# Turning gathered token rows through DRAM and VectorE instead of TensorE, from the third expert on

## The chip, the cores and the metric

The kernel runs on one core of a Trainium2 chip. The metric is the device time of one execution in microseconds (us); lower is better.

## What is computed

Sigmoid attention over 8 batches of 12 heads (448 tokens, head dimension 64), and then a mixture of 8 experts over the 3584 tokens of width 768. Each token goes to one expert; an expert holds at most 448 tokens, and the choice is greedy over all token-expert logits in descending order. Everything is float32.

```python
scores = scale * np.matmul(q, k.transpose(0, 1, 3, 2)) - np.log(S)
attn = 1.0 / (1.0 + np.exp(-scores))
x = np.matmul(attn, v)          # then transposed and reshaped to [3584, 768]
logits = x @ w_gate
...                             # greedy assignment, cap = N // E = 448
for e in range(E):
    mask = assigned == e
    h = np.maximum(x[mask] @ w1[e], 0.0)      # 768 -> 1024
    out[mask] = h @ w2[e]                     # 1024 -> 768
```

## The kernel before, in words

The first 275 us or so are attention (lines 363 to 531). Its rows are written to a DRAM tile `xs` of [3584, 768] (`rows`, L487 to L493). A router (class `Router`, L114 to L332) finds one full expert per phase: VectorE runs a search of 16 steps over the logits (L168 to L215), each step three counting instructions (L173) and a few small ones, and TensorE does small transposes and matmuls for it (L162, L224, L252, L257, L284, L291). A phase ends with the list of the expert's 448 tokens, `r_idx` (L293). The step numbered kx in the program is the expert found in phase kx; "expert 2" below is kx = 2, the third one.

For each expert the mixture stage then does this:

- `gather` (L616) reads the listed rows of `xs` into four SBUF tiles `xr` of up to 128 tokens (three of 128, one of 64) by indirect DMAs that GpSimd (POOL) issues.
- `xturn` (L621 to L636) turns them: channels have to lie on partitions for the matmul. Per tile and half of the channels, TensorE transposes three blocks of 128 channels into one PSUM tile `tp` (L632), ScalarE copies it, rounded, to `xh` (L635), and VectorE writes the remainder to `xl` (L636). That makes eight such groups per expert. A float32 product is made of three matmuls: high with high, low with high, high with low (L680, L682, L684; L715, L717, L719).
- `moe` (L660) runs the two weight stages. Stage 1 has four groups i of 256 hidden units, each made of two weight units (j = 0 uses channel blocks 0 to 2, j = 1 blocks 3 to 5). ScalarE evicts each group twice (L688 `hh`, L691 `yt`) and GpSimd writes the remainder `hl` (L692). Stage 2 has three groups of 256 output channels, evicted by ScalarE (L723). The PSUM pool `sc` has two buffers, so a third group can start only when the first has been evicted. `untranspose` (L641) turns the result back, two TensorE transposes per tile, with a ScalarE copy (L650), and GpSimd scatters finished rows (L653).
- Weights are streamed: `load_w` (L573) issues a DMA on the SP queue, three units ahead, and `split_w` (L592) makes the high part on ScalarE (L596) and the low part on GpSimd, for the last two experts on VectorE for every second unit (L598).

The order of the work is written out by the program, and each engine runs its own instructions strictly in that order. A generator `moe(kx)` yields after each matmul with an estimated cost; a clock adds these up. Routing steps are put in when the clock passes `t_route` (L772), and other pieces, the "chores", each with a due time, one per 1000 ns of that clock (L777 to L782). `prepare` (L752) makes the chores for the next expert as soon as its list has been emitted: gathers at `t0 + 1500 j`, turns later. `flush` runs what is left before the next expert begins.

```python
for j, n in blocks():
    for hf in range(2):
        chores.append((t0 + lag + 1500 * j, kx + 1,
                       lambda j=j, n=n, hf=hf: xturn(kx + 1, j, n, hf, False)))
```

Of the kernel before, what the change touches and what calls it, by code (L numbers as in the profile page):

```python
# [7 lines left out]
F32 = mybir.dt.float32  # L8
F32R = mybir.dt.float32r
# [4 lines left out]
AF = mybir.ActivationFunctionType  # L14
OP = mybir.AluOpType
# [3 lines left out]
STEP = 4.0e36  # L19
BIG = 16384.0  # L20
TWO23 = float(2 ** 23)
XR_BUFS = 12
XT_BUFS = 8
XA_BUFS = 4
AT_BUFS = 8
# [309 lines left out]
def moe_attention(tc, q, k, v, w_gate, w1, w2, out):  # L335
    nc = tc.nc
    B, H, S, D = q.shape
    DM = H * D
    E, _, F = w1.shape
    CP, NCH, NP, ND, NF = 112, S // 112, H // 2, DM // 128, F // 128  # L340
    G4 = 4
    PSUM = bass.MemoryType.PSUM
    with contextlib.ExitStack() as ctx:
# [229 lines left out]
        def load_w(u, behind=False):  # L573


            kx, st, i, j = units[u]
            if kx not in gate:
                gate[kx] = nc.sync.value_load(picked[kx][:1, :1], min_val=0, max_val=E - 1)
            t = wp.tile([128, 1024], F32, name="wr")
            if behind:  # L580
                nc.gpsimd.memset(t[:1, :1], 0.0)
            if st == 0:
                t = t[:, :768].rearrange("p (a f) -> p a f", a=3)
                src = w1[ds(gate[kx], 1)].rearrange("e (a p) f -> p (e a) f", p=128)
                nc.sync.dma_start(t, src[:, 3 * j:3 * j + 3, i * 256:(i + 1) * 256])
            else:
                t = t.rearrange("p (a f) -> p a f", a=4)
                src = w2[ds(gate[kx], 1)].rearrange("e (a p) f -> p (e a) f", p=128)
                nc.sync.dma_start(t, src[:, 4 * j:4 * j + 4, i * 256:(i + 1) * 256])
            raw[u] = t  # L590
# [17 lines left out]
                state["split"] += 1  # L608

        xg, XH = {}, {}  # L610

        def blocks():
            for j in range(4):
                yield j, min(128, S - 128 * j)

        def gather(kx, j, n):  # L616
            t = xg[kx, j] = xp.tile([128, DM], F32, name="xr", bufs=XR_BUFS)
            nc.gpsimd.indirect_dma_start(out=t[:n], out_offset=None, in_=xs,  # L618
                                         in_offset=bass.IndirectOffsetOnAxis(ap=listed[kx][:n, j:j + 1], axis=0))

        def xturn(kx, j, n, hf, wide):  # L621
            if (j, hf) == (0, 0):
                XH[kx] = (xp.tile([128, ND, S], F32R, name="xh", bufs=2),
                          xp.tile([128, ND, S], F32R, name="xl", bufs=2))
            xh, xl = XH[kx]
            if wide and hf:
                p = ps_s.tile([128, 2, 512], F32, name="sc")[:, 0]
            else:
                p = ps_t.tile([128, 512], F32, name="tp")
            for i in range(3):  # L630
                dd = hf * 3 + i
                nc.tensor.transpose(p[:, i * n:(i + 1) * n], xg[kx, j][:n, dd * 128:(dd + 1) * 128], ident[:n, :n])  # L632
            pv = p[:, :3 * n].rearrange("p (a t) -> p a t", a=3)
            sl = (slice(None), slice(hf * 3, hf * 3 + 3), slice(j * 128, j * 128 + n))
            nc.scalar.activation(xh[sl], pv, AF.Copy)  # L635
            nc.vector.tensor_tensor(xl[sl], pv, xh[sl].bitcast(F32), OP.subtract)  # L636
# [111 lines left out]
        for kx in range(E):  # L748
            turned = kx + 1 == E
            start = clock[0]  # L750

            def prepare():  # L752
                t0 = clock[0]
                lag = max(5000, min(14000, start + 40000 - t0))
                for j, n in blocks():
                    chores.append((t0 + 1500 * j, kx + 1, lambda j=j, n=n: gather(kx + 1, j, n)))
                for j, n in blocks():
                    for hf in range(2):
                        chores.append((t0 + lag + 1500 * j, kx + 1,
                                       lambda j=j, n=n, hf=hf: xturn(kx + 1, j, n, hf, False)))  # L760

            def flush(kx):
                for c in [c for c in chores if c[1] <= kx]:
                    chores.remove(c)
                    c[2]()

            for step, cost in enumerate(moe(kx)):
                clock[0] += cost
                t = clock[0]
                if kx == 0 and step == 35:  # L770
                    flush(0)
                if t >= t_route:  # L772
                    t_route = t + next(route, 0) + SLACK
                if not turned and kx + 1 in listed:
                    prepare()
                    turned = True
                if t >= t_chore:  # L777
                    c = next((c for c in chores if c[0] <= t), None)
                    if c:
                        chores.remove(c)  # L780
                        c[2]()
                        t_chore = t + CHORE_NS  # L782
            if not turned:
                while kx + 1 not in listed:
                    next(route)
                prepare()
            flush(kx + 1)
# [28 lines left out]
```

## Time and profile before

| what | us |
|---|---|
| three runs | 887.00, 890.27, 893.16 (median 890.27) |
| the profiled execution | 887.23 |
| its span, first to last instruction | 885.5 |
| mean granted TensorE clock | 0.984 |
| TensorE busy (PE) | 837.8 |
| VectorE busy (DVE) | 531.4 |
| ScalarE busy (ACT) | 456.2 |
| GpSimd busy (POOL) | 467.4 |

PE is matmul and transpose work, PEld the weight loads that overlap it, SP the queue that issues most DMAs. A row of the profile's timeline has the start, the duration, the engine, the line of the kernel, the operation, what it writes and reads, and, in brackets, how long the engine had been idle and what ended that. A row of the view of waits has what waited, for what, the total in us, the number of times and the longest. A row of the view by windows has the window, its length and, for each engine, the busy time and the number of instructions, then the granted clock, the share of time the DMA engines were busy and GB/s.

### The profile page before, as it was taken

To read this page: it belongs to the slowest core of one execution; us is meant where nothing else is said; L and a number is where in the kernel's file an instruction comes from. 1 tells how busy PE (TensorE), PEld (TensorE's weight loads), DVE (VectorE), ACT (ScalarE), POOL (GpSimd) and SP (SyncE) were. 2 spreads that over 40 slices of the span, in tenths; PEclk is the share of its full clock that TensorE was granted. 3 is DMA by queue.
4 is the path that set the end of the run, shared out by engine and by line. 5 is a ranking of instruction groups with operands and counts; after the bars stand their busy time and mean duration, and the time that the engine had idled before them with its cause. 6 is when DMAs were issued, how large, how long until landed. Compare 5 with 4: busy or idle time off the path is not lost.

```text
span 885.5 us, 16232 instructions
## 1 busy us (share of the span) xinstructions
PE 837.8 (95%) x5507; PEld 639.0 (72%) x5507; DVE 531.4 (60%) x2047; ACT 456.2 (52%) x610; POOL 467.4 (53%) x449
## 2 busy tenths in 40 slices
PE   6999999999998729998999999999999999999996
PEld 3455455455555518987988988988888888889996
DVE  4665555555554778958869779779689521421110
ACT  6777777777774724434424424434434434443431
POOL 9645444444400014846864964873883882752651
PEclk9999999999999969999999999999999999999999
DMA  9876666665603945434443542452552542632511
GB/s 172 168 144 127 132 125 123 131 126 120 138 12 100 299 161 153 136 107 161 136 133 117 146 156 75 157 164 95 153 164 70 178 146 72 228 111 72 192 49 63
DMA packets 203507, 117.57 MB, mean 133 GB/s; under 512 B 143936, under 2 KB 193088, under 8 KB 203424
## 3 DMA queue, kind: packets, MB, share of 16 engines
q1 hardware_dynamic: 190688, 83.03, 36.0%
q0 software_dynamic: 10880, 33.28, 11.9%
q8 instruction: 43, 0.70, 0.3%
q10 hardware_dynamic: 1856, 0.23, 0.2%
q14 instruction: 40, 0.33, 0.1%
HBM read 94.47 MB, written 22.02 MB: 132 GB/s over the span
## 4 chain that ended last, share of the span: by engine, by line
PE 77%; DVE 8%; DMA 5%; issue 4%; POOL 3%; ACT 1%; SPq 1%; POOLq 0%; ACTq 0%; DVEq 0%
PE tp L461 13%; PE sc L437 11%; PE sc L682 8%; PE sc L680 8%; PE sc L684 8%; PE sc L717 6%; PE sc L719 6%; PE sc L715 6%; PE tp L467 2%; DMA xs<-xr 2%; DVE r_junk L173 2%; PE sc L447 2%; PE tp L645 2%; DMA xr<-xs,r_idx 2%; PE tp L632 2%
## 5 line engine op out<-in xcount | busy, mean ns | idle before, releaser
L598 POOL TENSOR_TENSOR wl<-wr,wh 128x768 fp32r<-128x768 f32 (+1 forms) x96 | 205.9, 2155 | 134.6 <-ACT wh L596 126.9
L427 ACT ACTIVATE at<-sc,bias 128x896 f32<-128x896 f32 x168 | 161.0, 1006 | 63.1 <-PE sc L447 38.2
L372 POOL DMA_DIRECT2D nkq<-in_q_dram x188 | 118.6, 646 | 111.5 <-DVE kqT L412 104.7
L719 PE MATMUL sc<-hh,wl 128*128 128x448 f32 (+2 forms) x400 | 151.4, 378 | 0.0
L717 PE MATMUL sc<-hl,wh 128*128 128x448 f32 (+2 forms) x400 | 145.4, 364 | 0.1
L684 PE MATMUL sc<-xh,wl 128*128 128x448 f32 (+2 forms) x396 | 145.4, 367 | 0.0
L682 PE MATMUL sc<-xl,wh 128*128 128x448 f32 (+2 forms) x396 | 144.9, 366 | 0.0
L715 PE MATMUL sc<-hh,wh 128*128 128x448 f32 (+2 forms) x400 | 143.9, 360 | 0.0
L680 PE MATMUL sc<-xh,wh 128*128 128x448 f32 (+2 forms) x396 | 143.8, 363 | 0.0
L173 DVE TENSOR_SCALAR_CACHE_REDUCE r_junk<-r_KE,r_T 128x224 bf16<-128x224 f32 x315 | 123.2, 441 | 0.1
L461 PE MATMUL tp<-at,nv 128*64 128x448 f32 x576 | 118.8, 548 | 0.0
L596 ACT ACTIVATE wh<-wr 128x768 fp32r<-128x768 f32 (+1 forms) x112 | 102.0, 939 | 13.2 <-DMA wr<-in_moe_w_dram 13.1
L692 POOL TENSOR_TENSOR hl<-yt,hh 128x896 fp32r<-128x896 f32 x32 | 68.3, 2136 | 44.5 <-ACT yt L691 41.8
L421 DVE TENSOR_TENSOR kqL<-kqT,kqH 128x896 fp32r<-128x896 f32 (+1 forms) x49 | 52.6, 1073 | 58.3 <-ACT kqH L419 58.2
L688 ACT ACTIVATE hh<-sc 128x896 fp32r<-128x896 f32 x32 | 29.5, 920 | 111.0 <-PE sc L684 111.0
L618 POOL DMA_INDIRECT xr<-xs,r_idx x32 | 32.0, 1002 | 97.5 <-ACT wh L596 86.7
L717 PEld LDWEIGHTS sc<-hl,wh 128*128 128x128 f32 x400 | 75.2, 188 | 7.0 <-issue 1.1
L598 DVE TENSOR_TENSOR wl<-wr,wh 128x768 fp32r<-128x768 f32 (+1 forms) x16 | 25.1, 1571 | 91.7 <-ACT wh L596 91.5
L461 PEld LDWEIGHTS tp<-at,nv 128*64 128x64 f32 x576 | 37.1, 136 | 59.1 <-issue 57.9
L682 PEld LDWEIGHTS sc<-xl,wh 128*128 128x128 f32 x396 | 74.5, 188 | 6.3 <-issue 0.5
L715 PEld LDWEIGHTS sc<-hh,wh 128*128 128x128 f32 x400 | 75.6, 189 | 4.4
L680 PEld LDWEIGHTS sc<-xh,wh 128*128 128x128 f32 x396 | 74.7, 189 | 5.5
(156 smaller groups left out, 1323.7 us busy)
## 6 DMA issues: line engine op xcount, KB each, us to landing
wr<-in_moe_w_dram SPq DMA_DIRECT2D x64, 384.0 KB
wr<-in_moe_w_dram SPq DMA_DIRECT2D x48, 512.0 KB
xs<-xr SPq DMA_DIRECT2D x32, 336.0 KB
nkq<-in_k_dram SPq DMA_DIRECT2D x190, 56.0 KB
nkq<-in_q_dram POOLq DMA_DIRECT2D x188, 56.0 KB, 2.6
nv<-in_v_dram SPq DMA_DIRECT2D x92, 96.0 KB
nr<-in_v_dram SPq DMA_DIRECT2D x46, 32.0 KB
xr<-xs,r_idx POOLq DMA_INDIRECT x32, 4.4
```

Of the source, the lines that this page charges most:

```text
L173: nc.vector.tensor_scalar(junk, KE, T[:, i:i + 1].bitcast(F32), None, OP.is_ge, OP.add, accum_out=cnt[:, i:i + 1])
L372: qn.dma_start(t[o:o + 32, n], rws[x])
L427: nc.scalar.activation(a, p[:, :, :S], AF.Sigmoid, bias=bias, scale=1 / math.sqrt(D))
L461: nc.tensor.matmul(p[j * 64:j * 64 + 64, :S], nat["v", b, g][:, h0 + j, c, :], AT[b, pr, c][:, j, :], start=(c == 0), stop=(c == 2 and pr ...
L596: nc.scalar.activation(hi, raw[u], AF.Copy)
L598: eng.tensor_tensor(lo, raw[u], hi.bitcast(F32), OP.subtract)
L680: nc.tensor.matmul(ph[:, f, lo:hi], wh[:, a, fs], xh[:, dd, lo:hi], start=st, stop=False)
L682: nc.tensor.matmul(ph[:, f, lo:hi], wh[:, a, fs], xl[:, dd, lo:hi], start=False, stop=False)
L684: nc.tensor.matmul(ph[:, f, lo:hi], wl[:, a, fs], xh[:, dd, lo:hi], start=False, stop=en)
L715: nc.tensor.matmul(py[:, d2, :w], wh[:, a, dsl], h1, start=st, stop=False)
L717: nc.tensor.matmul(py[:, d2, :w], wh[:, a, dsl], h2, start=False, stop=False)
L719: nc.tensor.matmul(py[:, d2, :w], wl[:, a, dsl], h1, start=False, stop=(j == 1 and a == 3))
```

## The change

From expert 2 on (`if kx:` in `prepare`, which prepares kx + 1), the turn on TensorE is replaced by three new steps:

- `stage` writes each gathered tile to a DRAM tile `xq` (two of them, used in turn), by a DMA on the SP queue;
- `fetch` reads it back with four DMAs, also on SP: partition 32 i + c gets, for each block of 32 tokens, 192 channels of token c of the block. There are two fetches per expert, 8 blocks (256 tokens) and 6 blocks (192 tokens);
- `vturn` turns 32 x 32 pieces on VectorE, three instructions per fetch and channel half, whose source elements are 24 bytes apart; ScalarE copies the result from SBUF to `xh`, and VectorE writes the remainder `xl`.

So that both ways give the same layout, channel 6 p + a now lies on partition p of block a: the weight load of stage 1 takes its rows in that order, and the TensorE turn of experts 0 and 1 reads every sixth channel. The pool of row tiles shrinks from 12 to 10. The due times of the new chores are 6000 (write), 8500 (read, behind the second and fourth write), 13000 and 14500 (the halves' turns) behind the gather of the same tile.

```diff
-XR_BUFS = 12
+XR_BUFS = 10
...
-                src = w1[ds(gate[kx], 1)].rearrange("e (a p) f -> p (e a) f", p=128)
+                src = w1[ds(gate[kx], 1)].rearrange("e (p a) f -> p (e a) f", a=ND)
...
+        xq = [dr.tile([S, DM], F32, name=f"xq{i}") for i in range(2)]
...
+        def stage(kx, j, n):
+            nc.sync.dma_start(xq[kx % 2][j * 128:j * 128 + n], xg[kx, j][:n])
+
+        def fetch(kx, j0, j1):
+            t = xg[kx, 4 + j0] = xp.tile([128, 8, DM // 4], F32, name="xw", bufs=2)
+            v = xq[kx % 2].rearrange("(j c) (i w) -> i c j w", c=32, i=4)
+            for i in range(4):
+                nc.sync.dma_start(t[32 * i:32 * i + 32, :j1 - j0], v[i, :, j0:j1])
+
+        def vturn(kx, j0, j1, hf):
+            if (j0, hf) == (0, 0):
+                XH[kx] = (xp.tile([128, ND, S], F32R, name="xh", bufs=2),
+                          xp.tile([128, ND, S], F32R, name="xl", bufs=2))
+            xh, xl = XH[kx]
+            n = j1 - j0
+            w = xg[kx, 4 + j0].rearrange("p j (w a) -> p a j w", a=ND)
+            t = xp.tile([128, 3, 256], F32, name="xt", bufs=2)[:, :, :32 * n]
+            for a in range(3):
+                nc.vector.transpose(t[:, a].rearrange("p (j w) -> p j w", w=32), w[:, hf * 3 + a, :n])
+            sl = (slice(None), slice(hf * 3, hf * 3 + 3), slice(32 * j0, 32 * j1))
+            nc.scalar.activation(xh[sl], t, AF.Copy)
+            nc.vector.tensor_tensor(xl[sl], t, xh[sl].bitcast(F32), OP.subtract)
...
-                nc.tensor.transpose(p[:, i * n:(i + 1) * n], xg[kx, j][:n, dd * 128:(dd + 1) * 128], ident[:n, :n])
+                nc.tensor.transpose(p[:, i * n:(i + 1) * n], xg[kx, j][:n, dd::ND], ident[:n, :n])
...
+                if kx:
+                    for j, n in blocks():
+                        chores.append((t0 + 1500 * j + 6000, kx + 1, lambda j=j, n=n: stage(kx + 1, j, n)))
+                        if j % 2:
+                            r = (4 * j - 4, min(4 * j + 4, S // 32))
+                            t = t0 + 1500 * j + 8500
+                            chores.append((t, kx + 1, lambda r=r: fetch(kx + 1, *r)))
+                            for hf in range(2):
+                                chores.append((t + 4500 + 1500 * hf, kx + 1,
+                                               lambda r=r, hf=hf: vturn(kx + 1, *r, hf)))
+                    chores.sort(key=lambda c: c[0])
+                    return
```

**VectorE, expert 2, behind the search steps that follow its list.** `r_junk` rows are the counting of a search step, `xl` the remainders. Before, the last subtracts of eight, spread over the first search steps:

```order
676 L197 TENSOR_SCALAR r_j_6072,r_acc<-r_ct 128x3
677 L210 SCALAR_TENSOR_TENSOR r_T<-r_acc,rt 128x3
678 L212 TENSOR_SCALAR r_J<-r_acc,r_J 128x1
679 L636 TENSOR_TENSOR xl<-tp,xh 128x3x128
680 L636 TENSOR_TENSOR xl<-tp,xh 128x3x64
681 L173 TENSOR_SCALAR r_junk,c_CN<-r_KE,r_T 128x224 x3
```

and now, after the fifth step:

```order
683 L212 TENSOR_SCALAR r_J<-r_acc,r_J 128x1
684 L642 STREAM_TRANSPOSE xt<-xw 128x256 x3
685 L645 TENSOR_TENSOR xl<-xt,xh 128x3x256
686 L642 STREAM_TRANSPOSE xt<-xw 128x256 x3
687 L645 TENSOR_TENSOR xl<-xt,xh 128x3x256
688 L642 STREAM_TRANSPOSE xt<-xw 128x192 x3
689 L645 TENSOR_TENSOR xl<-xt,xh 128x3x192
690 L642 STREAM_TRANSPOSE xt<-xw 128x192 x3
691 L645 TENSOR_TENSOR xl<-xt,xh 128x3x192
692 L173 TENSOR_SCALAR r_junk,c_CN<-r_KE,r_T 128x224 x3
```

All four turns stand together between two steps here; for experts 3, 4 and 5 a search step stands behind the first and behind the second. For experts 6 and 7 they come when the search is over.

**SP's queue, expert 2, behind the loads of its first two weight units.** `wr` rows are weight loads. Before:

```order
136 L585 DMA wr<-in_moe_w_dram 128x3x256
137 L585 ISA
138 L585 DMA wr<-in_moe_w_dram 128x3x256
139 L585 ISA
140 L585 DMA wr<-in_moe_w_dram 128x3x256
```

and now:

```order
138 L585 DMA wr<-in_moe_w_dram 128x3x256
139 L624 DMA xq_3962<-xr 128x768 x2
140 L585 ISA
141 L585 DMA wr<-in_moe_w_dram 128x3x256
142 L624 DMA xq_3962<-xr 128x768
143 L631 DMA xw<-xq_3962 32x8x192 x4
144 L624 DMA xq_3962<-xr 64x768
145 L631 DMA xw<-xq_3962 32x6x192 x4
146 L585 ISA
147 L585 DMA wr<-in_moe_w_dram 128x3x256
```

The writes and reads of the rows stand between the second and the fourth weight unit of the same expert.

**ScalarE, expert 7's turns, in the first weight stage of expert 6.** `hh` and `yt` are the two evictions of a stage-1 group, `wh` the high parts of weights. Before:

```order
312 L688 ACTIVATE hh<-sc 128x896
313 L691 ACTIVATE yt<-sc 128x896
314 L596 ACTIVATE wh<-wr 128x768
315 L635 ACTIVATE xh<-tp 128x3x128 x3
316 L596 ACTIVATE wh<-wr 128x768
317 L635 ACTIVATE xh<-tp 128x3x128 x3
318 L688 ACTIVATE hh<-sc 128x896
```

and now:

```order
311 L714 ACTIVATE hh<-sc 128x896
312 L717 ACTIVATE yt<-sc 128x896
313 L596 ACTIVATE wh<-wr 128x768
314 L644 ACTIVATE xh<-xt 128x3x256
315 L596 ACTIVATE wh<-wr 128x768
316 L644 ACTIVATE xh<-xt 128x3x256
317 L644 ACTIVATE xh<-xt 128x3x192 x2
318 L714 ACTIVATE hh<-sc 128x896
319 L717 ACTIVATE yt<-sc 128x896
```

The eviction of the third group stands behind all four copies of expert 7 now, where two of the eight came later before.

## The prediction

> **What bounds the kernel now.** I read the span by experts first, then by routing phases, then the chain of waits on PE and VectorE, then single instructions. The window view, cut at the first matmul of experts 2, 3, 4 and 5 (the columns are length, then PE, PEld, DVE, ACT and POOL busy):
>
> ```profile
> 475.56:544.28 68.72, 67.47 (x379) 59.27 (x377) 57.30 (x298) 28.72 (x46) 45.34 (x30) 1.00 0.43 133
> 544.28:612.33 68.05, 67.75 (x383) 59.63 (x382) 55.07 (x300) 29.93 (x48) 45.42 (x30) 1.00 0.42 134
> 612.33:680.07 67.74, 67.30 (x377) 59.08 (x376) 55.90 (x303) 29.04 (x45) 46.31 (x30) 1.00 0.42 135
> 680.07:749.52 69.45, 69.38 (x415) 60.25 (x413) 27.16 (x112) 29.12 (x46) 45.09 (x29) 1.00 0.42 131
> ```
>
> PE is busy all but about 1 us of each expert, at full granted clock: whatever leaves PE's stream shortens an expert, unless PE then waits for another engine. VectorE is the engine to fear. The same view of VectorE alone, cut where the token lists of experts 2, 3, 4, 5 and 6 are written (L293), so one row is one routing phase:
>
> ```profile
> 456.47:518.91 62.44, 51.29 (x265) 1.00 0.45 140
> 518.91:581.71 62.80, 50.51 (x265) 1.00 0.42 132
> 581.71:643.61 61.90, 50.14 (x264) 1.00 0.41 131
> 643.61:705.89 62.28, 50.05 (x265) 1.00 0.43 138
> ```
>
> It works 50 to 51 us of 62.4. The 11 us left are no free time: most are waits inside a chain, and only the wait for PE's transpose of the threshold shows room. From VectorE's timeline, the first search step after the list of 456.47, two later ones, and that wait:
>
> ```profile
> 462.03 0.45 DVE L173 TENSOR_SCALAR_CACHE_REDUCE r_junk<-r_KE,c_c 128x224 bf16<-128x224 f32 x1
> ...
> 480.28 0.44 DVE L173 TENSOR_SCALAR_CACHE_REDUCE r_junk<-r_KE,r_T 128x224 bf16<-128x224 f32 x1
> ...
> 482.60 0.44 DVE L173 TENSOR_SCALAR_CACHE_REDUCE r_junk<-r_KE,r_T 128x224 bf16<-128x224 f32 x1
> ...
> 507.58 0.17 DVE L227 TENSOR_REDUCE r_km<-rt 112x1 f32<-112x8 f32 x1 [3.82 <-PE rt L224]
> ```
>
> Steps start 5.6 us behind the list and 2.3 us apart; at the end VectorE waits 3.8 us for PE. So a phase costs VectorE 62.4 - 3.8 = 58.6 us, and PE, which holds the routing's small matmuls at fixed places of its order, waits there when VectorE needs more.
>
> **What is removed.** 48 groups of three PE turns, eight for each of experts 2 to 7. Their price is read from the matmuls around them, a wide one and one of the 64-token block:
>
> ```profile
> 463.06 0.37 PE L717 MATMUL sc<-hl,wh 128*128 128x448 f32 x1
> 463.26 0.49 PE L632 MATMUL tp<-ident,xr 128*128 128x128 f32 x3
> 463.51 0.45 PE L719 MATMUL sc<-hh,wl 128*128 128x448 f32 x1
> 463.80 0.37 PE L715 MATMUL sc<-hh,wh 128*128 128x448 f32 x1
> 464.00 0.36 PE L717 MATMUL sc<-hl,wh 128*128 128x448 f32 x1
> ```
> ```profile
> 473.38 0.37 PE L717 MATMUL sc<-hl,wh 128*128 128x448 f32 x1
> 473.68 0.39 PE L632 MATMUL tp<-ident,xr 64*128 64x64 f32 x3
> 474.00 0.47 PE L719 MATMUL sc<-hh,wl 128*128 128x448 f32 x1
> ```
> ```profile
> PE tp L632 <- DVE xl L636: 3.2, 5, 0.9
> ```
>
> Matmuls start 0.20 us apart (463.80 to 464.00). Across a wide group two steps take 0.74 (463.06 to 463.80), 0.34 more; across a narrow one the first step takes 0.62, 0.42 more, and I add 0.1 for its second as with the wide one. 6 x 0.34 + 2 x 0.52 = 3.1 us per expert, 18.5 for six; with the 3.2 us that PE waited there for VectorE, 21.7 us, or 3.6 per expert. That is all there is to win.
>
> **What is added on VectorE.** Prices, from the groups by shape (mean ns stands behind the busy time), VectorE and then ScalarE:
>
> ```profile
> L412 DVE STREAM_TRANSPOSE kqT<-nkq 128x896 f32<-128x896 f32 x47 | 51.9, 1104 | 4.0 <-DMA nv<-in_v_dram 2.5 <-DMA nkq<-in_k_dram 0.8 <-issue 0.2
> ...
> L636 DVE TENSOR_TENSOR xl<-tp,xh 128x384 fp32r<-128x384 f32 x45 | 23.8, 551 | 19.6 <-ACT xh L635 19.4
> ...
> L598 DVE TENSOR_TENSOR wl<-wr,wh 128x768 fp32r<-128x768 f32 x10 | 15.3, 1541 | 52.7 <-ACT wh L596 52.5 <-issue 0.2
> ...
> L146 DVE TENSOR_REDUCE rt<-ML 112x32 f32<-112x256 f32 x7 | 4.2, 605 | 0.2
> ...
> L412 DVE STREAM_TRANSPOSE kqT<-nkq 128x448 f32<-128x448 f32 x2 | 1.3, 645 | 4.8 <-DMA nkq<-in_q_dram 4.0 <-DMA nkq<-in_k_dram 0.8
> ```
> ```profile
> L596 ACT ACTIVATE wh<-wr 128x768 fp32r<-128x768 f32 x64 | 52.7, 847 | 13.2 <-DMA wr<-in_moe_w_dram 13.1
> ```
>
> Transposes of 896 and 448 elements give 1.02 ns per element and 0.19 us fixed: 256 elements take 0.45, three 1.35 us; of 192, three take 1.16. The ScalarE copy of 768 takes 0.85. The subtract of 768 takes 1.1 at the rate of L636 (551 / 384), 1.54 by L598; I take 1.1, since the shape's twin L636 runs among the same neighbours. In the written order three transposes, the copy and the subtract stand one behind another, and VectorE waits for the copy: 3.3 us, less what neighbouring transposes overlap, 3.2; for 192, in proportion, 2.5. Two of each make 11.4 us per expert. The eight subtracts that go took 6 x 0.55 + 2 x 0.28 = 3.9. So VectorE's chain grows by 7.5 us, its floor per phase to 58.6 + 7.5 = 66.1 us, where PE, without turns, would need 62.4 - 3.6 = 58.8. Lower bound: were the copy hidden, 2.25 and 1.8, growth 4.2. Upper: source elements 24 bytes apart read as slowly as L146 does (605 / 256 = 2.4 ns per element) and subtracts at 1.54 give 4.2 and 3.2, growth 10.9.
>
> The Trainium skill, page "SBUF — State Buffer", section "Door 1: The DMA port swizzle", says that SBUF lines are 16 bytes and each access that crosses into a new one pays; a 24-byte step always crosses. By that rule the upper price holds, and the two early experts' weight loads of the new strided turns would also be slower; L146, with 64-byte steps, fits it, but no transpose or weight load here shows it. It is the third rival below.
>
> **What is added on the queues.** Per expert four writes and eight reads on SP's queue, behind gathers. Rows: the last gather of expert 2 on POOL, a gather's median landing, a write of rows to the same kind of DRAM tile:
>
> ```profile
> 465.53 0.91 POOL L618 DMA_INDIRECT xr<-xs,r_idx  x1
> ```
> ```profile
> xr<-xs,r_idx POOLq DMA_INDIRECT x32, 4.4
> ```
> ```profile
> 296.03 3.71 DMA xs<-xr
> ```
>
> 465.5 + 4.4 = 469.9, written 473.6, four reads issued by about 475 and landed (3.7 again) at 479; VectorE comes to that half at 456.5 + 5.6 + 5 x 2.3 + 2 x 3.2 = 480. The DMAs are just hidden behind VectorE for expert 2, by 1 us, so I cost them at nothing there; twice the latency would add some 7 us. SP waits for the gathers with weight loads behind it, but those load several units ahead, so nothing until expert 7. The changed w1 rows move the same bytes in the same runs: nothing.
>
> **The sum, by milestones.** Expert 2: list 456.5, VectorE at the turns 17.2 us later, first half of the channels complete after 3.2 + 3.2 + 2.5: 482.6. PE would be there at 475.56 - 3.6 = 472.0, so it loses 10.6 and expert 2 starts 7.0 late. Lists follow PE's place: list 3 at 518.91 + 7.0 = 525.9. Expert 3's turns have two search steps between them: list + 17.2 + 8.9 + 4.6 = list + 30.7 = 556.6, 12.3 late (PE itself: 547.7). List 4: 594.0; expert 4 at 624.7, 12.4 late (PE: 621.0). From there VectorE's floor: list 6 at 594.0 + 2 x 66.1 = 726.2 against 705.89, 20.3 late. Expert 6's turns come behind the last list, off the search, and are hidden; expert 6 starts 20.3 - 3.6 = 16.7 late.
>
> Expert 7 has a loss of its own. Its gathers go out while expert 6 runs. A gather's landing on the chain of waits, ScalarE's eviction of expert 6's third group, and PE's first second-stage matmul:
>
> ```profile
> 765.15 7.14 DMA xr<-xs,r_idx
> ```
> ```profile
> 774.94 0.92 ACT L688 ACTIVATE hh<-sc 128x896 fp32r<-128x896 f32 x1
> ```
> ```profile
> 783.10 0.36 PE L715 MATMUL sc<-hh,wh 128*128 128x448 f32 x1
> ```
>
> In the new order ScalarE's four copies for expert 7 stand ahead of that eviction. From expert 6's start (749.5): rows landed at +22.8, read back at about +27, then 3.2 per turn with a weight split between, and the fourth copy done at +39.3; eviction (0.92, twice) +41.1, where the PSUM pair comes free and PE could have begun at +33.6 - 3.6 = +30. Loss 11 (5 if the gather lands in 4.4 and the copies are hidden, 15 with the slow price). So 16.7 - 3.6 + 11 = 24.1 us late at the end. The profiled execution took 887.23 for its span of 885.5; 911.3 by it, and the median of the three runs is 3.0 above it: 914. With the lower bounds all through the same steps give +6, 896; with the upper ones +40, 930.
>
> **Rivals.** One: all of it is hidden. VectorE's idle 11 us take the added 7.5, PE gets its 21.7 back: 890.3 - 21.7 = 868.6. For it: PE's rows above are the bound, and lists 5 and 6 come 36 and 44 us before their experts start. Against: the order is fixed and the only wait with room is 3.8 us. It decides if the four turns take under 8 us per expert. Two: only the ends cost, expert 2's 10.6 and expert 7's 11, while the phases between slide into the lists' lead: 890.3 - 21.7 + 21.6 = 890. Against: PE's own routing matmuls wait for VectorE inside each expert, lead or not. Three: the strided source is slow in every transpose, and the subtracts beside POOL's work cost 1.54: 930; it decides from 0.6 us per transpose of 256.
>
> **Chances.** Forecast 0.58, hidden 0.13, ends only 0.10, slow stride 0.19. The three runs spread over 0.7%, so about 1% can be told from no change. The forecast's own range is 896 to 930; the low end of it lies within 1%, so 0.03 of it counts there. Faster 0.13, within 1% 0.13, slower 0.74. The range of 8 in 10 takes in the second and third rival and leaves out the first: 888 to 932.
>
> **What would show it.** Right: no PE turns for experts 2 to 7; PE idle before the first matmul of expert 2 and 3 by 5 to 11 us, ended by VectorE's xl or ScalarE's xh; the wait of 3.8 us at L227 gone and PE waiting for the threshold or ScalarE in the phases before lists 5 and 6; routing phases of 64 to 69 us; ScalarE's evictions late in expert 6. Wrong: phases at 59 us, or experts 3 to 6 near 64 us each; transposes of 256 at 0.6 us and over would speak for the third rival; first matmuls ended by a DMA would say that the round trip through DRAM, not VectorE, sets the pace.

## The result, and the profile after

The changed kernel takes 956.31 us (median of four runs, 954.34 to 957.88) against 890.05 us of the kernel before beside it: ratio 1.0742, 95% interval 1.0708 to 1.0775. It is slower, as forecast, but by 66.3 us where 24 were forecast, above the range. The profiled execution spans 956.1 us, at a mean granted clock of 0.943 (0.984 before).

The same view by experts as in the prediction, PE alone, cut at the first matmul of experts 2, 3, 4 and 5 (the last row ends where expert 6 begins):

```profile
488.28:566.72 78.44, 65.50 (x348) 0.91 0.50 151
566.72:643.74 77.02, 68.03 (x356) 0.92 0.47 151
643.74:725.59 81.85, 67.19 (x358) 0.91 0.48 148
725.59:803.24 77.65, 68.84 (x388) 0.93 0.49 153
```

These experts took 68 to 69 us, with at most 1.3 us of PE idle and the full clock; now they take 77 to 82, with 9 to 15 idle and 0.91 to 0.93 of the clock. VectorE by routing phases:

```profile
459.75:532.93 73.18, 57.17 (x272) 0.91 0.51 157
532.93:605.84 72.91, 56.43 (x272) 0.91 0.51 157
605.84:675.96 70.12, 55.94 (x272) 0.93 0.49 154
675.96:751.20 75.24, 55.97 (x272) 0.91 0.48 151
```

Its busy time grew by 6 us per phase; the prediction's prices without the waits for the copies make 2 x (1.35 + 1.1) + 2 x (1.16 + 0.83) - 3.9 = 5.0. But the phases grew from 62 us to between 70 and 75 (forecast 64 to 69). Where PE stood still, from its timeline:

```profile
488.28 0.74 PE L706 MATMUL sc<-xh,wh 128*128 128x448 f32 x1 [13.04 <-ACT xh L644]
...
566.72 0.74 PE L706 MATMUL sc<-xh,wh 128*128 128x448 f32 x1 [12.53 <-ACT xh L644]
...
716.66 0.69 PE L671 MATMUL tp<-ident,yt 128*128 128x128 f32 x2 [13.02 <-ACT xr L676]
```

and the wait that was to be used up, VectorE's for the threshold, in the phases of experts 3 and 5:

```profile
521.61 0.17 DVE L227 TENSOR_REDUCE r_km<-rt 112x1 f32<-112x8 f32 x1 [4.09 <-PE rt L224]
...
664.96 0.17 DVE L227 TENSOR_REDUCE r_km<-rt 112x1 f32<-112x8 f32 x1 [0.89 <-PE rt L224]
```

So PE waits for VectorE's turns in one place and VectorE still waits for PE in another. How the lateness gets to PE shows in the view of waits (who waits, total, times, longest):

```profile
ACT xh L644 <- DVE xt L642: 94.6, 24, 12.1
...
DVE xt L642 <- DMA xw<-xq: 34.9, 6, 14.0
...
PE sc L706 <- ACT xh L644: 25.6, 2, 13.0
...
PE tp L671 <- ACT xr L676: 24.0, 5, 13.0
...
ACT wh L596 <- DMA wr<-in_moe_w_dram: 19.3, 4, 10.1
```

ScalarE stands 94.6 us before its 24 copies, and behind them in its order stand its own evictions, which PE needs. PE's clock falls in such a wait; around the one that ends at 488.28 (window, length and PE busy, clock):

```profile
475.25:488.28 13.03, 0.00 (x0) 0.60 0.59 175
488.28:490.28 2.00, 1.95 (x5) 0.50 0.00 2
490.28:492.28 2.00, 2.00 (x9) 0.66 0.00 0
492.28:494.28 2.00, 2.00 (x13) 1.00 0.00 0
```

The next 4 us run at 0.50 and 0.66: 2 x 0.50 + 2 x 0.34 = 1.7 us lost behind the wait itself. PE's bracketed waits from 335 us on add up to 6.7 us before and 75.7 after, 69.0 more. The two profiled executions differ by 956.1 - 885.5 = 70.6 us, so the waits alone make nearly all of it, and something else used up what the removed turns gave back. PE alone from 335 us to the end, before and after:

```profile
335.00:885.50 550.50, 536.43 (x3039) 1.00 0.40 128
```
```profile
335.00:956.10 621.10, 538.27 (x2895) 0.93 0.45 141
```

PE is busy 1.8 us longer with 18.5 us of turns less to do, so 20.3 us went to slower work. Restarts behind nine waits of over 3 us explain some 15 of it (9 x 1.7, an estimate from the one shown). The rest is not broken down; the slower weight loads shown below may be part of it.

### The profile page after: what moved, and what is told of

Its sections match the earlier page's. It is cut to its first block, busy times and chain, and to the rows that moved or that the text cites. A ratio compares the mean times of both kernels' runs of the same rounds, so it can differ in the third digit from the quotient of the medians.

```text
span 956.1 us, 16057 instructions
## 1 busy us (share of the span) xinstructions
PE 838.0 (88%) x5363; PEld 639.7 (67%) x5363; DVE 562.8 (59%) x2095; ACT 452.9 (47%) x586; POOL 467.4 (49%) x449
## 4 chain that ended last, share of the span: by engine, by line
PE 62%; DVE 11%; issue 8%; DMA 8%; POOL 6%; ACT 3%; SPq 2%; POOLq 0%; DVEq 0%; ACTq 0%
PE tp L461 12%; PE sc L437 10%; PE sc L706 7%; PE sc L708 7%; PE sc L710 7%; PE sc L745 4%; PE sc L743 4%; PE sc L741 3%; DMA xw<-xq 3%; DVE xt L642 3%; POOL wl L598 3%; DVE r_junk L173 2%; PE tp L467 2%; PE sc L447 2%; PE tp L671 2%
## 5 line engine op out<-in xcount | busy, mean ns | idle before, releaser
L706 PE MATMUL sc<-xh,wh 128*128 128x448 f32 (+2 forms) x396 | 147.8, 373 | 30.9 <-ACT xh L644 25.6
L741 PE MATMUL sc<-hh,wh 128*128 128x448 f32 (+2 forms) x400 | 147.5, 369 | 5.6 <-ACT wh L596 5.6
L743 PE MATMUL sc<-hl,wh 128*128 128x448 f32 (+2 forms) x400 | 148.1, 370 | 0.1
L708 PE MATMUL sc<-xl,wh 128*128 128x448 f32 (+2 forms) x396 | 147.7, 373 | 0.1
L706 PEld LDWEIGHTS sc<-xh,wh 128*128 128x128 f32 x396 | 77.1, 195 | 37.8 <-ACT xh L644 26.3
L741 PEld LDWEIGHTS sc<-hh,wh 128*128 128x128 f32 x400 | 77.7, 194 | 11.3 <-ACT wh L596 6.0
L745 PEld LDWEIGHTS sc<-hh,wl 128*128 128x128 f32 x400 | 77.3, 193 | 9.0 <-POOL wl L598 4.0
L708 PEld LDWEIGHTS sc<-xl,wh 128*128 128x128 f32 x396 | 76.7, 194 | 6.8 <-DVE xl L645 0.5
L710 PEld LDWEIGHTS sc<-xh,wl 128*128 128x128 f32 x396 | 76.6, 193 | 5.8 <-DVE wl L598 0.6
L598 DVE TENSOR_TENSOR wl<-wr,wh 128x768 fp32r<-128x768 f32 (+1 forms) x16 | 22.1, 1384 | 97.3 <-ACT wh L596 97.1
```

The costliest lines, as they stand in the source:

```text
L598: eng.tensor_tensor(lo, raw[u], hi.bitcast(F32), OP.subtract)
L706: nc.tensor.matmul(ph[:, f, lo:hi], wh[:, a, fs], xh[:, dd, lo:hi], start=st, stop=False)
L708: nc.tensor.matmul(ph[:, f, lo:hi], wh[:, a, fs], xl[:, dd, lo:hi], start=False, stop=False)
L710: nc.tensor.matmul(ph[:, f, lo:hi], wl[:, a, fs], xh[:, dd, lo:hi], start=False, stop=en)
L741: nc.tensor.matmul(py[:, d2, :w], wh[:, a, dsl], h1, start=st, stop=False)
L743: nc.tensor.matmul(py[:, d2, :w], wh[:, a, dsl], h2, start=False, stop=False)
```

## The experiments

ORDER below is the theory that VectorE's turns and ScalarE's copies in their written places stop PE; TRIP that the rows come back from DRAM too late; QUEUE that weight loads stand on SP behind writes that wait for gathers; FLOOR that VectorE's own length paces the phases. Other names are explained in the expectation that uses them. The edits show the lines that matter; lines between them are left out, some marked by `...`. Each run has the kernel before beside it, at 889.8 to 891.5 us.

**VectorE makes the first copy.**

```diff
-            nc.scalar.activation(xh[sl], t, AF.Copy)
+            nc.vector.tensor_copy(xh[sl], t)
```

> The four copies to xh of each expert from the third on are done by VectorE in the place where it waited for ScalarE; all else as in the changed kernel. Theory ORDER (VectorE turns late, and ScalarE's four copies, standing in ScalarE's order ahead of PSUM evictions and waiting for VectorE, stop PE): the PE waits on ScalarE's xr copies and yt copies (24.0 + 8.4 us) and most of the 17 us of expert 7 go, the waits at the start of experts 2 and 3 (13 us each) stay: 910 to 930. Theory TRIP (the round trip through DRAM and SP's queue make the rows late, whoever copies): 945 to 957. Theory STRIDE (24-byte steps): 950 to 957.

Measured: 948.83 us, ratio 1.0688 [1.0644, 1.0732]: far above ORDER's range and inside TRIP's, which the turns alone (below) speak against. VectorE's copy takes 0.95 us where it had waited 0.83 for ScalarE's (19.9 us for 24), so a turn is hardly longer. Some waits of PE behind ScalarE's copies went, but the phases stay at 70 to 76 us, and PE waits for VectorE's search in addition:

```profile
736.65 0.46 PE L224 MATMUL rt<-ident,r_kap 128*112 128x128 f32 x1 [8.09 <-DVE r_kap L217]
```

**The new order of channels, all turns on TensorE.**

```diff
-                if kx:
+                if kx > 8:
```

> All experts are turned by TensorE as before the change, but in the new channel layout (every sixth channel in the weight load of the turn, stage-1 weight rows in the new order, 10 row tiles). ORDER: only the strided loads cost; list 2 came 3.3 us later with two experts turned so, eight of them give at most 13: 890 to 903. STRIDE: the layout itself carries much of the loss: over 920. TRIP: no round trip, so near 890.

Measured: 895.09, ratio 1.0060 [1.0041, 1.0079]. Costed at nothing, it takes 5.2 us. TensorE's weight loads of its turns, before and in the changed kernel's early experts (count, then shortest, median and longest in ns):

```profile
L632 PEld LDWEIGHTS tp<-ident,xr x180: 134/140/231, 331.7 to 777.5; 128*128 128x128 f32 x135, 64*128 64x128 f32 x45
```
```profile
L658 PEld LDWEIGHTS tp<-ident,xr x36: 207/233/242, 331.8 to 409.8; 128*128 128x128 f32 x27, 64*128 64x128 f32 x9
```

Reading every sixth element takes them from 140 to 233 ns. Experts 2 to 6 grow by 0.4 to 0.8 us each in this run. The changed kernel has such turns in its first two experts alone, so its share should be below 5.2; the new order of w1 in DRAM wasn't tried apart from the turns.

**Rows fetched without waiting for the write.** Fixed rows of `xs` are read in place of the staged ones, so that other tokens than the listed ones are multiplied.

```diff
-            v = xq[kx % 2].rearrange("(j c) (i w) -> i c j w", c=32, i=4)
+            v = xs[kx * S:(kx + 1) * S].rearrange("(j c) (i w) -> i c j w", c=32, i=4)
```

> The reads of the rows take fixed rows of xs, so that they wait neither for a gather nor for a write (the writes are still made, nothing reads them; the tokens are not the listed ones). Theory ORDER: VectorE's 35 us of waiting for these reads go, mostly those of experts 6 and 7, but experts 2 to 5 are still turned at the same places of the order: 925 to 940. Theory TRIP: nearly all of the loss goes: 880 to 905. STRIDE: 925 to 945.

Measured: 954.66, ratio 1.0741 [1.0708, 1.0773], outside every range named and the same as the changed kernel. The write's own landing costs next to nothing. It does not test the whole trip: the fetches still stand on SP behind writes that wait for gathers.

**The new way from expert 4 on.**

```diff
-                if kx:
+                if kx >= 3:
```

> Experts 2 and 3 are turned by TensorE too (strided), the new way begins with expert 4, whose list comes about 30 us ahead of its start. ORDER: the two waits of 13 us at the starts of experts 2 and 3 go, and the waits behind ScalarE's copies in experts 3 to 6 stay (9.0 + 14.7 + 8.8 + 14.4 us and the clock's recovery), less 3.6 us of turns per expert: 920 to 935. If a lead of 30 us is enough to hide all: 875 to 888.

Measured: 936.89, ratio 1.0543 [1.0511, 1.0575], just above ORDER's range. Leaving out experts 2 and 3, whose starts had the 13 us waits, gives back 19 us; 47 are lost in the rest, though these lists come 30 us and more before their experts.

**The turns alone.** No write, no read: VectorE turns a block loaded once, so the listed rows are not what is multiplied. All other places stay.

```diff
-            w = xg[kx, 4 + j0].rearrange("p j (w a) -> p a j w", a=ND)
+            w = xg[0, 4 + j0].rearrange("p j (w a) -> p a j w", a=ND)
...
+        fetch(0, 0, 8)
+        fetch(0, 8, S // 32)
...
-                        chores.append((t0 + 1500 * j + 6000, kx + 1, lambda j=j, n=n: stage(kx + 1, j, n)))
...
-                            chores.append((t, kx + 1, lambda r=r: fetch(kx + 1, *r)))
```

> No DMA of the new way is left: the stages and fetches are gone and VectorE turns a block of rows that was loaded once, so the gathered rows are not what is multiplied from the third expert on. SP waits for no gather and VectorE's transposes for no DMA; the gathers themselves, the turns, ScalarE's copies and their places stay. ORDER (VectorE's chain and ScalarE's copies in their written places stop PE): the stalls at the starts of experts 2 and 3 stay at 9 to 13 us each, those inside experts 3 to 5 stay, only expert 7's loss shrinks, since no weight stands behind a gather: 925 to 945. TRIP (the rows come back from DRAM too late): the stalls at starts and in expert 6 go, 880 to 900. Half of each would be 905 to 920.

Measured: 932.53, ratio 1.0465 [1.0429, 1.0500], and the waits at the starts are still there:

```profile
487.90 0.74 PE L706 MATMUL sc<-xh,wh 128*128 128x448 f32 x1 [11.25 <-ACT xh L644]
...
565.48 0.74 PE L706 MATMUL sc<-xh,wh 128*128 128x448 f32 x1 [10.42 <-ACT xh L644]
```

With no write or read left to wait for, 932.53 - 891.46 = 41.1 us stay. TRIP can't explain this share; ORDER or FLOOR can. No run has the turns without their 24-byte steps, so what the steps add to it is not separated.

**The DMAs alone, first as chores, then beside them.** Both issue every write and read, and TensorE turns the gathered rows. In the first they take places in the paced list; in the second they go out at their due times.

```diff
-                            for hf in range(2):
-                                chores.append((t + 4500 + 1500 * hf, kx + 1,
-                                               lambda r=r, hf=hf: vturn(kx + 1, *r, hf)))
-                    chores.sort(key=lambda c: c[0])
-                    return
```
```diff
-                        chores.append((t0 + 1500 * j + 6000, kx + 1, lambda j=j, n=n: stage(kx + 1, j, n)))
+                        free.append((t0 + 1500 * j + 6000, kx + 1, lambda j=j, n=n: stage(kx + 1, j, n)))
...
-                            chores.append((t, kx + 1, lambda r=r: fetch(kx + 1, *r)))
...
+                            free.append((t, kx + 1, lambda r=r: fetch(kx + 1, *r)))
...
+                while free and free[0][0] <= t:
+                    free.pop(0)[2]()
                 if t >= t_chore:
```

> All writes and reads of the new way are issued in their places, but nothing reads what comes back: TensorE turns the gathered rows, as in the run of the layout alone (895). ORDER: the DMAs cost nothing at the starts of experts; only the second-stage weights of expert 6 and the first of expert 7 stand behind the four gathers on SP's queue: 898 to 908, with all of the growth in expert 6. TRIP does not act here, nothing waits for the rows. QUEUE (writes that wait on SP hold up the weights of every expert): 910 to 930, with PE or ScalarE waiting for weights in experts 2 to 5 too.

> The DMAs alone (TensorE turns the gathered rows) cost 933.8, but there the six new entries per expert also took places in the paced list of chores and pushed TensorE's turns to the expert's end. Here the writes and reads go out at their due times beside the list, so that the turns stand where they stood in the layout run (895.1). QUEUE: 912 to 930, ScalarE still waits for weights in experts 4 to 6. CROWDING (the pushed turns made the loss): 895 to 905.

Measured: 933.77, ratio 1.0481 [1.0432, 1.0530], and 919.62, ratio 1.0339 [1.0308, 1.0371]. The first lies above every range named, but there the turns were also pushed to the experts' ends; in the second they stand where they stood in the layout run. Its experts 3 to 6:

```profile
547.38:616.07 68.69, 68.37 (x383) 1.00 0.58 179
616.07:688.70 72.63, 69.20 (x377) 0.98 0.54 169
688.70:764.99 76.29, 71.65 (x415) 0.98 0.48 150
764.99:843.20 78.21, 67.71 (x338) 0.91 0.49 157
```

Nothing is lost up to expert 3; in experts 4, 5 and 6 it is 4, 6 and 13 us against the layout run (68.30, 70.26 and 64.93). ScalarE's splits wait there for weights, which they did not in these experts before:

```profile
732.50 1.06 ACT L596 ACTIVATE wh<-wr 128x1024 fp32r<-128x1024 f32 x1 [7.44 <-DMA wr<-in_moe_w_dram]
...
793.30 0.84 ACT L596 ACTIVATE wh<-wr 128x768 fp32r<-128x768 f32 x1 [10.89 <-DMA wr<-in_moe_w_dram]
```

SP's queue in expert 6 of this run shows why (`xq<-xr` is a write of rows):

```profile
757.76 0.37 SPq L585 DMA_DIRECT2D wr<-in_moe_w_dram  x1
772.65 0.35 SPq L624 DMA_DIRECT2D xq<-xr  x1
773.26 0.37 SPq L585 DMA_DIRECT2D wr<-in_moe_w_dram  x1
```

The write waits for its gather, and for 15 us no weight load is issued. QUEUE holds: 919.62 - 895.09 = 24.5 us. The turns alone and the DMAs alone, 41.1 + 24.5 = 65.6, come close to the 66.3 of the whole change. That they match so well may be chance: in the changed kernel VectorE also waits 14.0 and 12.3 us for the rows of experts 6 and 7, which happens in neither of the two runs, and waits can overlap.

**The turns later, from expert 4 on.**

```diff
-                if kx:
+                if kx >= 3:
-                                chores.append((t + 4500 + 1500 * hf, kx + 1,
+                                chores.append((t + 12500 + 1500 * hf, kx + 1,
```

> As the run with the new way from expert 4 on (936.9), but the four turns of an expert become due 8 us later in PE's time, so that fewer of ScalarE's copies stand ahead of the untransposes' evictions while VectorE is still in its search. ORDER: the stalls inside experts 4 and 5 (9.1, 12.7, 6.1 us there) shrink by half, expert 6's stays: 920 to 930. If it is not the place but VectorE's total that paces the phases (FLOOR), the time goes from one stall to another: 932 to 940.

Measured: 933.38, ratio 1.0473 [1.0436, 1.0509], 3.5 us under the run with the turns as they were. The waits inside experts shrank and came back at the starts (8.33 and 7.41 us at experts 4 and 5), and the time lies in FLOOR's range.

**The turns alone, right behind the list, with ScalarE's copy and then with VectorE's.**

```diff
-                                chores.append((t + 4500 + 1500 * hf, kx + 1,
+                                chores.append((t - 10000 + 1500 * hf, kx + 1,
```

> The turns alone (932.5; a block of rows that was loaded once is turned, not the gathered ones), but due 14.5 us earlier, right behind the list, as no real rows could be. PLACE (the stall at each start comes because the turns stand a gather and a round trip behind the list): the stalls at the starts of experts 2 and 3 go, 900 to 915. FLOOR (VectorE's growth of 8 us per phase is what PE waits for, wherever it stands): 922 to 935, phases still at 66 us and more.

> The turns alone and due right behind the list (929.4; a block of rows that was loaded once is turned), with the first copy made by VectorE instead of ScalarE. There PE waited 9.8, 8.7, 7.7 and 5.1 us for evictions that stand behind ScalarE's copies, while VectorE waited 3 to 5 us per phase for PE's transpose of the threshold. SCALAR (ScalarE's copies carry VectorE's lateness to PE, and VectorE's own growth would fit into its slack): these stalls go and the phases fall to 62 to 66 us, 893 to 908. FLOOR (VectorE's growth itself makes the phases longer, whoever carries it to PE): phases stay at 68 to 71, 918 to 932.

Measured: 929.38, ratio 1.0434 [1.0401, 1.0466], and 932.95, ratio 1.0495 [1.0471, 1.0518]. With the turns early the waits left the starts and came up at the evictions behind ScalarE's copies:

```profile
486.01 0.69 PE L671 MATMUL tp<-ident,yt 128*128 128x128 f32 x2 [9.77 <-ACT xr L676]
```

With the copy on VectorE these went too, and PE waits for the search itself, while VectorE's wait for the threshold is used up at last:

```profile
590.33 0.46 PE L224 MATMUL rt<-ident,r_kap 128*112 128x128 f32 x1 [11.56 <-DVE r_kap L217]
...
733.33 0.46 PE L224 MATMUL rt<-ident,r_kap 128*112 128x128 f32 x1 [12.70 <-DVE r_kap L217]
```
```profile
590.82 0.17 DVE L227 TENSOR_REDUCE r_km<-rt 112x1 f32<-112x8 f32 x1 [0.55 <-PE rt L224]
```

Its phases take 69 to 74 us, and its time lies 1 us above FLOOR's range. Some of its subtracts are slow, up to 3.1 us where the changed kernel's take 0.96, for a reason that no run shows:

```profile
537.35 3.08 DVE L645 TENSOR_TENSOR xl<-xt,xh 128x768 fp32r<-128x768 f32 x1
```

PLACE and SCALAR are out all the same: the wait only changes its place, and in the last run it is VectorE's search, made longer by the turns, that PE waits for.

**The writes and reads on POOL's queue.**

```diff
-            nc.sync.dma_start(xq[kx % 2][j * 128:j * 128 + n], xg[kx, j][:n])
+            nc.gpsimd.dma_start(xq[kx % 2][j * 128:j * 128 + n], xg[kx, j][:n])
-                nc.sync.dma_start(t[32 * i:32 * i + 32, :j1 - j0], v[i, :, j0:j1])
+                nc.gpsimd.dma_start(t[32 * i:32 * i + 32, :j1 - j0], v[i, :, j0:j1])
```

> The changed kernel with its writes and reads issued from POOL instead of SP, so that no weight load stands behind a gather; POOL, with 45 of 68 us busy, waits for the gathers instead. QUEUE (a large part of the loss is weights that come late to ScalarE): 930 to 942, about what the turns alone cost (932.5), and expert 7's weights in time. ORDER alone (VectorE's turns explain nearly all): 945 to 956. If POOL's own work becomes late (its splits of weights stand behind the waits): above 956.

Measured: 989.16, ratio 1.1110 [1.1074, 1.1146], the outcome named last. POOL spends 0.59 us on each read it issues and 31.4 us in front of them:

```profile
L631 POOL DMA_DIRECT2D xw<-xq x48 | 27.9, 589 | 42.4 <-DMA xq<-xr 31.4 <-issue 11.1
```

Its weight splits come late behind that, so the run tells nothing for or against QUEUE.

**The last two experts alone,** with w1 and TensorE's turns of the others as before, VectorE copying, writes and reads on SP and then on POOL.

```diff
-                if kx:
+                if kx >= 5:
-            nc.scalar.activation(xh[sl], t, AF.Copy)
+            nc.vector.tensor_copy(xh[sl], t)
-                src = w1[ds(gate[kx], 1)].rearrange("e (p a) f -> p (e a) f", a=ND)
+                src = w1[ds(gate[kx], 1)].rearrange("e (p a) f -> p (e a) f" if kx >= 6 else "e (a p) f -> p (e a) f", a=ND)
```

> The new way for experts 6 and 7 alone, where VectorE has no search left, w1 and the turns of the other experts as in the kernel before, and VectorE makes the first copy too, so that ScalarE's evictions wait for nothing new. 12 turns groups fewer on PE are worth 7 us at most. ORDER: no stall at the start of expert 6 (44 us of lead), expert 7 still loses 8 to 12 us, since its weights stand behind the gathers on SP: 888 to 898. TRIP or QUEUE for every expert: a stall at the start of expert 6 too, 900 to 910. If expert 7's loss came from ScalarE's copies alone: 881 to 885.

> The run with the new way for experts 6 and 7 alone (908.4), its writes and reads on POOL instead of SP. There ScalarE waited 8.0, 6.4 and 5.7 us for second-stage weights behind the writes. QUEUE: those waits go and with them the stall before expert 6 and most of expert 7's loss: 884 to 892. If the loss of these two has another cause (the turns' place, VectorE's split of weights, POOL): 898 to 910.

Measured: 908.38, ratio 1.0216 [1.0167, 1.0265], and 915.51, ratio 1.0283 [1.0255, 1.0311]. No search is left beside these turns, and still the first loses 17 us, in the range of TRIP or QUEUE. The second lies above both its ranges: ScalarE waits for no weights in its last experts, but POOL, which now waits for the gathers, splits the weights late:

```profile
792.12 0.74 PE L710 MATMUL sc<-xh,wl 128*128 128x448 f32 x1 [9.64 <-POOL wl L598]
```

It too tells nothing for or against QUEUE. SP's queue and ScalarE in expert 5 of the first run:

```profile
721.68 0.35 SPq L624 DMA_DIRECT2D xq<-xr  x1
725.70 0.34 SPq L624 DMA_DIRECT2D xq<-xr  x1
729.17 1.81 SPq L631 DMA_DIRECT2D xw<-xq  x4
731.20 0.40 SPq L589 DMA_DIRECT2D wr<-in_moe_w_dram  x1
```
```profile
728.21 1.06 ACT L596 ACTIVATE wh<-wr 128x1024 fp32r<-128x1024 f32 x1 [8.00 <-DMA wr<-in_moe_w_dram]
...
736.50 1.06 ACT L596 ACTIVATE wh<-wr 128x1024 fp32r<-128x1024 f32 x1 [6.36 <-DMA wr<-in_moe_w_dram]
```

The weight load of 731.20 stands behind two writes, issued 4 us apart as their gathers land, and reads that wait for them.

**The same with writes, reads and turns later,** for the last two experts, for expert 7 alone (`kx >= 6`, and the new order of w1 from 7 on), and for both with expert 6's pieces a little earlier (17000, 22000 and 500 below).

```diff
-                        chores.append((t0 + 1500 * j + 6000, kx + 1, lambda j=j, n=n: stage(kx + 1, j, n)))
+                        chores.append((t0 + 1500 * j + 20000, kx + 1, lambda j=j, n=n: stage(kx + 1, j, n)))
-                            t = t0 + 1500 * j + 8500
+                            t = t0 + 1500 * j + 26000
-                                chores.append((t + 4500 + 1500 * hf, kx + 1,
+                                chores.append((t + 5500 + 1500 * hf, kx + 1,
```

> The run with the new way for experts 6 and 7 alone (908.4), its writes due 14 us, its reads 17.5 us and its turns 18.5 us later in PE's time, still ahead of the expert that needs them, so that the gathers have landed before SP comes to the writes and SP holds up no weight. QUEUE (all that the new way loses in the last two experts is SP waiting for gathers): 882 to 888, no wait of ScalarE for weights above 2 us, and faster than before by the 7 us of turns. If 10 us or more stay, something else is lost there: 895 to 910.

> The same for expert 7 alone, so experts 0 to 6 are those of the kernel before. Expert 7's gathers are the late ones (a landing at 22.8 us after expert 6's start). QUEUE: 884 to 890, a gain of at most 3.6. If the gathers are still not down when SP comes to the writes, first-stage weights of expert 7 come late: 895 to 903, and then the loss of the run above lies in expert 7 too.

> The run with the last two experts' DMAs later (889.3, as before) still lost 4.2 us at the start of expert 6: VectorE stood behind a split of weights (a wait of 22.9 us for ScalarE) while the rows were back. Here expert 6's writes, reads and turns are due 3, 4 and 9 us earlier, which puts three of its four turns ahead of that split; the gathers are still down before SP's writes. QUEUE and the turns' price together: that stall goes below 1 us and the time is 883 to 886, 4 to 7 us under the kernel before. If the writes wait for gathers again: 889 to 895.

Measured: 889.34, ratio 1.0000 [0.9985, 1.0016]; 886.86, ratio 0.9969 [0.9957, 0.9981]; and 885.46, ratio 0.9943 [0.9921, 0.9965]. The waits for weights are gone, and 19 us come back with them, as QUEUE has it. The turns were moved too, though, and VectorE's waits for rows (13.6 and 10.9 us in the run of 908.38, with weight splits of its own behind them) went at the same time; what each is worth is not separated here, and QUEUE alone is shown by the DMAs alone. The first missed its 882 to 888 for a named reason: expert 6's turns stood on VectorE behind a weight split that waited for ScalarE, and PE lost 4.2 us at the start.

```profile
743.82 0.96 DVE L598 TENSOR_TENSOR wl<-wr,wh 128x768 fp32r<-128x768 f32 x1 [22.92 <-ACT wh L596]
```
```profile
754.17 0.47 PE L706 MATMUL sc<-xh,wh 128*128 128x448 f32 x1 [4.20 <-DVE xh L644]
```

The third puts three of the four turns ahead of that split and is 4.4 us under the kernel before: there most of the 7 us of turns is kept.

## Why the prediction was wrong

Right were the sign, the gain and the price. The gain: in the run with expert 7 alone, expert 6, which holds those turns, takes 61.09 us against 64.57, 3.5 for the forecast 3.6. The price: one turn of expert 2, VectorE's rows,

```profile
482.79 1.64 DVE L642 STREAM_TRANSPOSE xt<-xw 128x256 f32<-128x256 f32 x3
485.34 0.96 DVE L645 TENSOR_TENSOR xl<-xt,xh 128x768 fp32r<-128x768 f32 x1 [0.91 <-ACT xh L644]
486.22 1.29 DVE L642 STREAM_TRANSPOSE xt<-xw 128x192 f32<-128x192 f32 x3
```

is 486.22 - 482.79 = 3.4 us, and the narrower one 2.7: 12.3 per expert for the forecast 11.4. That the total came so close is partly luck. The transposes by shape (count, then busy time and mean ns):

```profile
L642 DVE STREAM_TRANSPOSE xt<-xw 128x256 f32<-128x256 f32 x36 | 20.0, 607 | 34.9 <-DMA xw<-xq 34.9
```

A strided transpose of 256 takes 0.61 us where 0.45 was the estimate for adjacent elements from rows of the same kind; three of them overlap and take 1.64. So the prediction's sign for the slow stride, 0.6 us and over, was there. The rival's price (growth 10.9 us per phase) was not, since the subtract took 0.96 us, less than the forecast's 1.1 and far less than the rival's 1.54; the dearer transposes and the cheaper subtract made up for each other in part. By the rule of the Trainium skill that the prediction cited ("SBUF — State Buffer", "Door 1: The DMA port swizzle"), strided reads pay; the trace agrees for weight loads (140 to 233 ns) and for transposes (0.61 us against the estimate of 0.45).

The stalls before experts 2 and 3 were forecast too, at 5 to 11 us and ended by `xl` or `xh`; they were 13.0 and 12.5, ended by `xh`.

**The step "the wait of 3.8 us at L227 gone" failed first.** The floor of 66.1 us per phase let the added work take that wait's place. In the changed kernel the phases without this wait are 73.18 - 4.1 = 69.1 and 70.12 - 0.9 = 69.2, 3 us over the floor: 0.9 for the turns, 1.2 and 2.0 that their first transpose waited for rows, and up to 0.9 of other waits. And the wait itself stayed at 3.5 to 4.1 us in three of the four phases, since PE had lost its time further up: it stood 13 us for ScalarE's copies, behind which its own evictions or its next expert's rows stood, and so came late to the transpose that VectorE waits for. Where ScalarE carries nothing and the turns come early (the run of 932.95), that wait is 0.4 to 0.6 us, which bears this out. Here two engines waited for each other in turn at two places, and both waits were paid. From list 2 to list 6 that made 751.20 - 459.75 = 291.4 us, 42.0 over the four phases of before; forecast were 726.2 - 456.5 = 269.7, 20.3 over. Expert 6 started 803.24 - 749.52 = 53.7 us late, 3.3 of them already there at list 2, where the forecast had 16.7. The place of the copies carried the lateness to PE, but the runs with VectorE's copy (948.83 and 932.95) lost about as much, and where no search stands beside the turns, in the last two experts, a gain came in the end: VectorE's length during the search is the cause that stays.

**"SP waits for the gathers with weight loads behind it, but those load several units ahead, so nothing until expert 7" failed next,** with 24.5 us where the forecast put nothing (its loss of 11 in expert 6 was for ScalarE's copies). Four writes each wait for a gather that lands 4.3 us after its issue, and POOL issues the gathers 1.3 to 6.6 us apart between its own work. The lists come earlier and earlier in an expert: in the run of the DMAs alone 37 us behind the start of expert 3, then 31 and 26 behind those of experts 4 and 5, whose second weight stages begin 33 us behind their starts. So from expert 4 on the writes hold up loads that the running expert itself needs next; SP issued none from 646.71 to 664.93, and expert 4's second stage began at 648.77.

**The new order of channels** stands in the sum at nothing: the prediction looked at the transfer of w1's rows there, and named the slower weight loads of TensorE's strided turns only beside the third rival. Both together cost 5.2 us if TensorE makes all the turns.

**Missing altogether was PE's clock:** a long wait takes more after it, 1.7 us behind the one shown. The Trainium skill, "TensorE: Matmul & The Clock Gate", section "What's actually happening", says that an idle window of about 3.4 us halves the clock and as much activity restores it. The rows at 488 to 492 us agree in kind (0.50, then 0.66, then 1.00). Its remark in the same section that the ramp penalty is under 1% of a typical kernel span is made for the warm-up at a kernel's start; here, with nine long waits, some 15 us of 956 are 1.6%.

The DMA round trip was forecast as hidden by 1 us for expert 2, and VectorE waited 1.2 us for it there, a small miss. But it waited 1.2, 2.0 and 4.2 us for the rows of experts 3 to 5, and 14.0 us for those of expert 6, which were forecast as hidden. Expert 5, in which these last turns stand, takes 77.65 us in the changed kernel and 69.16 with the turns alone, so nearly all that it loses comes with the DMAs.

## What to carry to other kernels

When work is moved from a full engine to one with idle time, look at where that idle time lies. Here a wait of 3.8 us inside a chain did not absorb work put further up in the chain, and an engine that runs in order and carries the result (ScalarE's copies) handed each delay on to whatever stood behind it. A DMA that waited for another DMA held up the loads behind it on SP's queue, once for 15 us; issuing it when the first had landed, with the turns later too, took this change for two experts from 908 to 889 us. Add PE's slow restart, 1.7 us in the stretch shown, to the price of a wait of several us.

## What was not expected of the hardware

VectorE's 32 x 32 transposes with source elements 24 bytes apart take a third longer than the estimate for adjacent ones (0.61 against 0.45 us for 256), while TensorE's weight loads with the same step take two thirds longer (140 to 233 ns). A read issued from POOL's queue keeps POOL for 0.59 us (48 of them, 27.9 us); moving the 72 writes and reads from SP to POOL made the changed kernel 33 us slower.
